# Attention front of a fused attention and two-layer MoE kernel: the order of small steps around the softmax sums, and the first inverse root moved to GpSimd

## Chip, cores and metric

One core of a Trainium2 chip (trn2) runs the whole program. The metric is the device time of one execution in microseconds. The kernel before took 538.94 us (median of 3 runs, 538.9 to 538.95).

## The reference, cut to what matters

```python
def _attn_ref(q, k, v, cap):                 # 2 x 12 heads, 448 positions, 64 wide
    scores = cap * np.tanh(scale * q @ k.T / cap)
    attn = np.exp(scores - max)
    attn = attn / (np.sum(attn, axis=-1, keepdims=True) + 1e-09)
    return attn @ v
def _moe_ref(x, w_gate, w_val, w_out, rms_g):      # x: 896 tokens x 768
    rms = np.sqrt(np.mean(x * x, axis=-1, keepdims=True) + 1e-06)
    xn = x / rms * rms_g
    return silu(xn @ w_gate) * (xn @ w_val) @ w_out
# followed by _moe2_ref: prelu(x @ w_in) @ w_out
```

The change touches the attention, and the `1 / rms` of the first batch of 448 tokens.

## The kernel before, in words

Everything is kept transposed: features on partitions, 448 tokens of a batch on the free axis. The attention is a loop over 12 head pairs (`NPAIR`), six for each batch, called **steps 0 to 11** here; step *i* computes the scores of pair *i* and finishes pair *i-1*. The order on every engine is the order in which the code calls the functions (`manual_schedule`); nothing is reordered. Each score operand is split in a high and a low part (`hi`, `lo`), so that three passes of matmuls give near full precision.

One step, by engine:

- TensorE (PE): `evac_o` frees a bank for it; then `qk_tail` (L207), `qk` for three groups (L221), `sums` of the pair before (L277: sums of the exponentials by a matrix of ones, and part of the values), `pv` of the pair before (L251). In even steps from 4 on, `norms` (L378) puts two `spread` matmuls (L372) behind the first `qk` group: they broadcast the inverse sums `r2` of two finished pairs into two banks, and `scaled` (L376) multiplies the kept values `ee` by them on VectorE, into `xf`. In step 8 the two stand ahead of the `qk` groups.
- The two banks that `spread` fills are single buffers: `under()` (tile tag u) is free once `evac_u`'s copy (L327) of the step before is done, `upper()` (tag o) once `evac_o`'s copy `ee` (L319), the first thing VectorE does in a step, is done.
- ScalarE (ACT): tanh and exp of the scores (L240, L243), and some of the weight conversion (`w_top`, L117).
- VectorE (DVE): `ee`, then `scaled`, then the lists described next, then `evac_u` (L327).
- GpSimd (POOL): sums of weight blocks (`w_sum`, L130) and, in `square` (L352 to L360), the running sum of squares of `xf`.
- SyncE (SP): issues the loads (`load_raw`, `load_v`, `w_load`), the two small DMAs `gt` of `evac_u` (L330) and the two small DMAs `r` of `recip` (L345).

Two lists per step, filled ahead of the loop, hold the rest: `first[i]` runs behind the step's softmax, `second[i]` at its end. `first` holds the loads, `prep(i+1)` (L189, two DVE instructions that split the next pair's operands), `recip` in odd steps (L332: four small DVE instructions on 64 partitions x 28, behind the landing of `gt`), and `w_bits` (L119). Before, `recip` stands behind `prep` in steps 3, 5 and 7 and ahead of it in steps 9 and 11:

```python
            steps = [(prep, i + 1)]
            if i % 2 == 1 and i > 2:
                steps.insert(i < 9, (recip, (i - 3) // 2))
```

The first batch's inverse root goes: in step 9, behind `qk_tail`, `rms_sum(0)` sums the squares over partitions on PE (L397, two matmuls into `upper("ms")`), VectorE copies the result out (L571), ScalarE takes the square root (`rms_root`, L404, with its table loaded for it and the tanh table loaded again behind it), and in step 10 VectorE takes the reciprocal (`rms_tail`, L407). `xnorm` (L418) uses the result from step 11 on. In step 10, `sums` of pair 9 stands ahead of the last `qk` group; in all other steps behind it.

Weight sums on GpSimd: `sum1` and `sum2` of group 0 and `sum1` of group 1 in steps 6 and 7; in step 8 the squares of pairs 4 and 5, then `sum2` of group 1 and `sum3` of groups 0 and 1; in step 10 the squares of pairs 6 and 7, then `sum4` of group 0.

Behind the attention, from about 97 us on, the dense layers follow (`product`, L449 and on), and PE goes from matmul to matmul to the end.

Of the kernel before, what the change touches and what calls it, by code (L numbers as in the profile page):

```python
# [7 lines left out]
F32 = mybir.dt.float32  # L8
F32R = mybir.dt.float32r
F16 = mybir.dt.float16  # L10
BF16 = mybir.dt.bfloat16
U16 = mybir.dt.uint16
U32 = mybir.dt.uint32
AF = mybir.ActivationFunctionType
ALU = mybir.AluOpType
PSUM = bass.MemoryType.PSUM
# [2 lines left out]
B, H, S, D = 2, 12, 448, 64  # L19
NP = H // 2  # L20
DM = H * D
# [12 lines left out]
RMS_EPS = 1e-6  # L34
SM_EPS = 1e-9
RP = 16
Q = 32
# [20 lines left out]
def attn_moe_kernel(ctx: ExitStack, tc: tile.TileContext, units, qk_in, v, sel, w, gvec, alpha, out):  # L58
    nc = tc.nc
# [7 lines left out]
    aconst = att.enter_context(tc.tile_pool(name="aconst", bufs=1))  # L67
    sb = att.enter_context(tc.tile_pool(name="sb", bufs=2))
# [11 lines left out]
    ones = aconst.tile([P, P], F32, name="ones")  # L80
    sel_t = aconst.tile([P, P], F32R, name="sel_t")
    r2 = [aconst.tile([P, S], F32R, name=f"r2_{i}") for i in range(2)]

# [4 lines left out]
    UW = UK * P  # L90
    tops = [const.tile([P, UW], U32, name=f"top{i}") for i in range(2)]
    raw_t, f_t, h_t, l_t = {}, {}, {}, {}
# [26 lines left out]
    def w_bits(u):  # L119
        n = width(u)  # L120
        f_t[u] = f_tile(u)[:, :n]
        nc.vector.scalar_tensor_tensor(  # L122
            out=f_t[u].bitcast(U32), in0=raw_t.pop(u).bitcast(U32)[:, 1:2 * n + 1:2], scalar=13,
            in1=top_of.pop(u), op0=ALU.logical_shift_right, op1=ALU.bitwise_or,
# [79 lines left out]
    def third():  # L204
        return ps_x.tile([P, 2, 512], F32, tag="x", name="s")
# [27 lines left out]
    def soft(i):  # L233
        t = pt[i] = sb.tile([P, TILES, S], F32, tag="pt", name="pt")
        done = 0
        for g in (*range(TG), TG) if i == 0 else (TG, *range(TG)):
            part = t[:, 2 * g:2 * g + 2] if g < TG else t[:, 2 * TG]
            if g == TG and split[i]:
                part = part.rearrange("p (h s) -> p h s", h=2)
            nc.scalar.activation(out=part, in_=st.pop((i, g)), func=AF.Tanh, scale=cinv)  # L240
            if (i, g) == (0, 1) or g == (TG if i == 0 else TG - 1):
                to = 4 if (i, g) == (0, 1) else TILES
                nc.scalar.activation(out=t[:, done:to], in_=t[:, done:to], func=AF.Exp, scale=cap_t)  # L243
                done = to
# [3 lines left out]
    def upper(name):  # L248
        return ps_o.tile([P, 512], F32, tag="o", name=name)
# [27 lines left out]
    def sums(i):  # L277

        t = pt[i]
        if i == last:  # L280
            us[i], oo[i] = (ps_s.tile([P, 2, 512], F32, tag="s", name=x)[:, 0] for x in ("us", "oo"))
        else:
            us[i] = under()
            if i:
                oo[i] = upper("oo")

        def add(h, x, k, m=slice(0, P), src=None):
            q = h + 2 * x
            nc.tensor.matmul(  # L289
                us[i][q * Q:q * Q + Q, HALF[0]], ones[m, :Q], t[m, k, src or HALF[x]], start=k == 2 * TG,  # L290
                stop=k // 2 == TG - 1, skip_group_check=True,
            )

        pv_tail(i, False)
        for h in range(2):
            for x in range(2):
                if split[i]:
                    add(h, x, 2 * TG, HEAD[x], HALF[h])
                else:
                    add(h, x, 2 * TG, HEAD[h])  # L300
        if i == 0 and split[i]:
            pv_tail(i, True)
        for n in range(2 * TG):
            for x in range(2):
                add(n % 2, x, n)
        if i and split[i]:
            pv_tail(i, True)
# [13 lines left out]
    def evac_u(i, queues=(nc.sync, nc.sync)):  # L321

        n, j = group[i]
        if j == 0:
            gt[n] = sb.tile([4 * RP, S // RP], F32, tag="gt", name="gt")
        u = sb.tile([P, S // 2], F32, tag="us", name="us")
        nc.vector.tensor_copy(u, us.pop(i)[:, HALF[0]])  # L327
        for h, q in enumerate(queues):
            r0 = 2 * RP * j + RP * h
            q.dma_start(out=gt[n][r0:r0 + RP], in_=u[h * Q:P:D].rearrange("x (p s) -> x p s", p=RP // 2))  # L330
# [16 lines left out]
    def square(i):  # L347
# [5 lines left out]
        else:  # L353
# [3 lines left out]
            else:  # L357
                nc.scalar.activation(out=sq, in_=x, func=AF.Square)
            if i < NPAIR - 2:
# [6 lines left out]
    def under():  # L366
        return ps_r.tile([P, 512], F32, tag="u", name="rps")
# [10 lines left out]
    def norms(i, *to):  # L378
        for fn in (spread, scaled):
            for j, rps in enumerate(to):  # L380
                fn(i + j, rps)
# [7 lines left out]
    rstd, spare = {}, {}  # L389

    ms_of = {}

    def rms_sum(b, ms):
        ms_of[b] = ms
        parts = s2.pop(b)
        for n, t in enumerate(parts):
            nc.tensor.matmul(ms[:, :S], ones, t, start=n == 0, stop=n == len(parts) - 1)  # L397

    def rms_keep(b):
        spare[b] = xpool.tile([P, K3, S], F32, tag="B22h", name="spare")  # L400
        rstd[b] = spare[b][:, 2]

    def rms_root(b):
        nc.scalar.activation(out=rstd[b], in_=ms_of.pop(b)[:, :S], func=AF.Sqrt, scale=1.0 / DM, bias=rms_b)  # L404

    def rms_tail(b):
        nc.vector.reciprocal(out=rstd[b], in_=rstd[b])  # L407


    oper = {}  # L410

    def first_operand(name):
# [54 lines left out]
    with tc.manual_schedule():  # L467
# [5 lines left out]
        nc.vector.memset(rms_b, RMS_EPS)  # L473
        for t in tops:
            nc.vector.memset(t, 0)
        for t in r2:
            nc.vector.memset(t.bitcast(F32), 0.0)
        hi[0] = sb.tile([P, QM], F32R, tag="hi", name="hi")
        r = sb.tile([P, QK + 1], F32, tag="rw", name="rw", bufs=2)
# [32 lines left out]
        def a(i, fn, *args):  # L512
            first.setdefault(i, []).append((fn, args))

        def z(i, fn, *args):
            second.setdefault(i, []).append((fn, args))
# [8 lines left out]
        for i in range(NPAIR):  # L525
            a(i, load_raw, i + 2)
            a(i, load_v, i + 1)
            if i == 1:
                for put, u in zip((a, z), conv[1:RAW]):
                    put(i, w_load, u)  # L530
            steps = [(prep, i + 1)]
            if i % 2 == 1 and i > 2:
                steps.insert(i < 9, (recip, (i - 3) // 2))
            for step in steps:
                a(i, *step)
            if i - 2 in range(len(conv)):
                a(i, w_bits, conv[i - 2])
                if i - 2 < len(conv) - RAW:
                    a(i, w_next, conv[i - 2])
            if i % 2 == 0 and i > 2:  # L540
                for j in range(2):
                    (a if i == 8 else z)(i, square, i - 4 + j)
            if i - 1 in range(len(conv)):
                if i < 5:
                    z(i, w_top, conv[i - 1], nc.vector.tensor_copy)
                else:
                    a(i, w_top, conv[i - 1])
        a(9, rms_root, 0)
        for n, j in ((3, 0), (4, 1), (9, 6)):
            z(n, w_hi, conv[j], nc.vector.tensor_copy)  # L550
            (a if n == 9 else z)(n + (n == 9), w_lo, conv[j])
        a(11, w_hi, conv[7])
        for put, n, fn, g in ((z, 6, sum1, 0), (z, 7, sum1, 1), (z, 7, sum2, 0), (a, 8, sum2, 1), (a, 8, sum3, 0),
                              (z, 8, sum3, 1), (z, 10, sum4, 0)):
            put(n, fn, "g", g)
        z(10, rms_tail, 0)
        a(11, xnorm, K3)
        z(11, xnorm, K3 + 1)
        for i in range(NPAIR):
            pairs = i % 2 == 0 and i > 2  # L560
            if i > 2:
                evac_o(i - 2)
            if i:
                home = {1: (ps_r, "u"), 2: (ps_o, "o")}.get(i)
                qk(i, TG, home[0].tile([P, 1, 512], F32, tag=home[1], name="s") if home else third())
            if i == 8:
                norms(i - 4, under(), upper("rps"))
            if i == 9:
                rms_sum(0, upper("ms"))
                rms_keep(0)  # L570
                nc.vector.tensor_copy(rstd[0], ms_of[0][:, :S])  # L571
                ms_of[0] = rstd[0]
            two = lambda: ps_s.tile([P, 2, 512], F32, tag="s", name="s")
            for g in range(TG - 1):
                qk(i, g, two())
                if pairs and i != 8 and g == 0:
                    norms(i - 4, under(), upper("rps"))
                if (i, g) == (1, 0):
                    oo[0] = upper("oo")
                    pv(0, range(2))  # L580
            if i == 0:
                qk(0, TG - 1, third())
                qk(0, TG, two())
            if i == 1:
                pv(0, range(2, TG))
            if i == 10:
                sums(i - 1)
            if i:
                qk(i, TG - 1, third())
            soft(i)  # L590
            for fn, args in first.pop(i, []):
                fn(*args)
            if i and i != 10:
                sums(i - 1)
            if i == 1:
                evac_o(0)
            if i:
                evac_u(i - 1)
                if i > 1:
                    pv(i - 1)  # L600
                del pt[i - 1], hi[i - 1], lo[i - 1], vt[i - 1]
            for fn, args in second.pop(i, []):
                fn(*args)
# [743 lines left out]
```

## Time and profile before

| what | value |
|---|---|
| median of 3 runs | 538.94 us |
| the profiled execution, its own time | 538.46 us |
| span of its instructions | 536.7 us |
| PE busy | 529.5 us (99%) |
| DVE, ACT, POOL busy | 448.4, 401.2, 112.0 us |

The span leaves 1.8 us around it. PE is the engine to look at: its busy time and its idle time together are the span, so the kernel is shorter only where PE waits less or does less. An idle engine beside it costs nothing until PE, or something in PE's way, waits for it.

### The profile page before, as it was taken

How to read it: one execution, taken by the hardware profiler on the slowest of the kernel's cores; microseconds unless marked ns; L12 is line 12 of the kernel's file. 1: busy time of each engine (PE TensorE's matmuls, PEld its weight loads, DVE VectorE, ACT ScalarE, POOL GpSimd, SP SyncE). 2: the span in 40 equal slices, each digit the busy share in tenths (PEclk: the TensorE clock that was granted, in tenths of full speed). 3: DMA queues.
4: the chain of work that ended last, by engine and by line, in shares of the span. 5: the costliest groups of instructions: out<-in, count | busy, mean ns of one | idle time of the engine just before them, and what ended most of it. 6: DMA issues, size and time to landing. Idle time of an engine off the chain costs nothing.

```text
span 536.7 us, 8344 instructions
## 1 busy us (share of the span) xinstructions
PE 529.5 (99%) x3322; PEld 450.9 (84%) x3322; DVE 448.4 (84%) x516; ACT 401.2 (75%) x475; POOL 112.0 (21%) x80
## 2 busy tenths in 40 slices
PE   8999999999999999999999999999999999999997
PEld 5554544799999999999999999999999999999996
DVE  5588889898999968789789796959997897998951
ACT  7989989577766665477788776789989996995530
POOL 0023763400066441010023011110310131210000
PEclk9999999999999999999999999999999999999999
DMA  6856520400334526048866769334466689564111
GB/s 213 317 174 228 180 77 11 160 18 2 117 118 176 174 87 211 0 177 253 274 179 111 165 205 299 66 59 131 174 231 230 207 233 203 97 144 112 51 53 51
DMA packets 22343, 80.05 MB, mean 149 GB/s; under 512 B 3744, under 2 KB 6688, under 8 KB 22304
## 3 DMA queue, kind: packets, MB, share of 16 engines
q1 hardware_dynamic: 16378, 65.43, 35.2%
q0 software_dynamic: 5552, 13.70, 14.0%
q8 instruction: 26, 0.43, 0.3%
q10 hardware_dynamic: 374, 0.39, 0.2%
q14 instruction: 13, 0.11, 0.1%
HBM read 62.99 MB, written 2.75 MB: 123 GB/s over the span
## 4 chain that ended last, share of the span: by engine, by line
PE 89%; DVE 5%; ACT 2%; POOL 2%; DMA 1%; issue 0%; DVEq 0%; SPq 0%
PE s L449 19%; PE x L449 13%; PE m L449 13%; PE s L825 8%; PE x L825 7%; PE s L795 6%; PE x L795 5%; PE m L825 4%; PE m L795 3%; PE oo L256 2%; PE s L229 2%; PE rps L289 2%; PE s L461 1%; ACT pt L243 1%; PE oo L272 1%; DVE wt L122 1%
## 5 line engine op out<-in xcount | busy, mean ns | idle before, releaser
L143 DVE TENSOR_TENSOR wl<-wt,wh 128x768 fp32r<-128x768 f32 x109 | 111.7, 1026 | 20.4 <-ACT wh L137 20.1
L137 ACT CAST wh<-wt 128x768 fp32r<-128x768 f32 x106 | 87.9, 832 | 39.8 <-PE s L825 9.1
L130 POOL TENSOR_TENSOR wt<-wt 128x768 f32<-128x768 f32 x25 | 58.4, 2341 | 163.6 <-DVE wl L143 75.7
L117 ACT CAST top<-raw 128x768 f16<-128x768 bf16 x64 | 68.9, 1077 | 20.2 <-DMA raw<-w_in 9.0
L122 DVE SCALAR_TENSOR_TENSOR wt<-raw,top 128x768 uint32<-128x768 uint32 x64 | 66.9, 1047 | 1.1 <-ACT top L117 1.1
L449 PE MATMUL s<-xx,wh 128*128 128x448 f32 x264 | 63.7, 365 | 0.0
L671 DVE TENSOR_TENSOR xx<-b,xx 128x896 fp32r<-128x896 f32 (+1 forms) x55 | 62.3, 1139 | 0.0
L449 PEld LDWEIGHTS s<-xx,wh 128*128 128x128 f32 x264 | 49.3, 187 | 4.8 <-issue 0.9
L449 PE MATMUL x<-xx,wh 128*128 128x448 f32 x204 | 49.9, 366 | 0.0
L449 PE MATMUL m<-xx,wh 128*128 128x448 f32 x204 | 49.5, 364 | 0.0
L892 POOL DMA_DIRECT2D wt<-wt x25 | 22.0, 880 | 126.1 <-DVE wt L122 62.6
L240 ACT ACTIVATE pt<-s,cinv 128x896 f32<-128x896 f32 (+1 forms) x48 | 41.0, 911 | 4.6 <-PE s L229 2.3
L449 PEld LDWEIGHTS x<-xx,wh 128*128 128x128 f32 x204 | 38.2, 187 | 3.5 <-issue 0.4
L825 PE MATMUL s<-xx,wh 128*128 128x448 f32 x144 | 40.9, 364 | 0.0
L449 PEld LDWEIGHTS m<-xx,wh 128*128 128x128 f32 x204 | 38.2, 187 | 3.0
L825 PE MATMUL x<-xx,wh 128*128 128x448 f32 x128 | 36.3, 364 | 0.0
L243 ACT ACTIVATE pt<-pt,cap_t 128x3136 f32<-128x3136 f32 (+2 forms) x13 | 35.3, 2714 | 0.4
L449 PE MATMUL s<-xx,wl 128*128 128x448 f32 x132 | 33.8, 364 | 0.0
L795 PE MATMUL s<-xx,wh 128*128 128x448 f32 x108 | 30.7, 364 | 0.0
L256 PE MATMUL oo<-pt,vt 128*32 128x448 f32 x288 | 29.5, 540 | 0.4 <-ACT pt L243 0.4
L825 PEld LDWEIGHTS s<-xx,wh 128*128 128x128 f32 x144 | 27.0, 188 | 1.9
L1186 ACT CAST xx<-b 128x896 fp32r<-128x896 f32 x28 | 26.4, 943 | 1.2 <-DVE b L671 1.1
(204 smaller groups left out, 1122.7 us busy)
## 6 DMA issues: line engine op xcount, KB each, us to landing
raw<-w_in SPq DMA_DIRECT2D x68, 768.0 KB
wt<-wt POOLq DMA_DIRECT2D x25, 384.0 KB, 4.7
rw<-qk_in SPq DMA_DIRECT2D x11, 480.0 KB
vt<-v_in SPq DMA_DIRECT2D x12, 288.0 KB
lent<-wt POOLq DMA_DIRECT2D x5, 384.0 KB, 7.5
b<-b POOLq DMA_DIRECT2D x4, 448.0 KB, 5.7
out<-P SPq DMA_DIRECT2D x5, 224.0 KB
out<-b SPq DMA_DIRECT2D x2, 448.0 KB
```

The costliest lines, as they stand in the source:

```text
L117: copy(top_of[u].bitcast(F16)[:, 1::2], raw_t[u].bitcast(BF16)[:, 4:4 * n + 4:4])
L122: nc.vector.scalar_tensor_tensor(out=f_t[u].bitcast(U32), in0=raw_t.pop(u).bitcast(U32)[:, 1:2 * n + 1:2], scalar=13, in1=top_of.pop(u), o ...
L130: add(out=t, in0=f_t[a], in1=f_t[b], op=op)
L137: copy(h_t[u], f_t[u].rearrange("p (k m) -> p k m", m=P))
L143: nc.vector.tensor_tensor(out=l_t[u], in0=f_t[u].rearrange("p (k m) -> p k m", m=P), in1=h_t[u], op=ALU.subtract)
L240: nc.scalar.activation(out=part, in_=st.pop((i, g)), func=AF.Tanh, scale=cinv)
L243: nc.scalar.activation(out=t[:, done:to], in_=t[:, done:to], func=AF.Exp, scale=cap_t)
L256: nc.tensor.matmul(oo[i][q * Q:q * Q + Q, :S], vv[:, n, q % 2 * Q:q % 2 * Q + Q], t[:, n, :], start=i == c == 0, stop=i > 0 and c == TG - ...
L449: nc.tensor.matmul(ps[:, r, :S], lhs, rhs, start=first and n == 0, stop=n == len(mm) - 1, skip_group_check=True,)
L671: nc.vector.tensor_tensor(out=out, in0=a, in1=b, op=op)
L795: nc.tensor.matmul(dst[m], wt[:, kk * MB + m, :], x, start=first and u == 0 and kk == 0 and n == 0, stop=u == UO - 1 and kk == 1 and n == ...
L825: nc.tensor.matmul(dst[m], wt[:, kk * MB + m, :], x, start=first and u == kk == i == 0, stop=last and kk == 1 and i == 2, skip_group_check ...
```

## The change

Step numbers as above. It

- puts `recip` ahead of `prep` in steps 3, 5 and 7 too;
- in step 6 puts `sums(5)` and `evac_u(5)` ahead of `w_bits` (on PE their place stays; on VectorE and SyncE they come earlier);
- in step 10 puts `sums(9)` back behind the last `qk` group;
- on GpSimd moves `sum2` of group 0 from step 7 to step 8, behind the squares, and `sum3` of group 1 to step 9;
- in step 9 puts `rms_sum(0)` behind the first `qk` group, and in place of the copy, the square root on ScalarE and the reciprocal on VectorE: a copy of 32 rows (`root_begin`), a DMA of one row to a tile of 16 partitions x 28, a scale on GpSimd, two integer instructions on VectorE (the usual first guess of an inverse root), four Newton steps of four instructions on GpSimd, the split in two parts there, and four DMAs from SyncE to rows of a new tile `rr` (`root_small`, at the start of `second[9]`, ahead of `sum3` of group 1 on GpSimd);
- in step 11, behind the first `qk` group, broadcasts `rr` by one matmul and copies it out on VectorE (`root_end`);
- clears `rr` once at the start on VectorE.

```diff
+    rr = aconst.tile([D, S], F32R, name="rr")
...
+    def root_begin(ms):
+        u = sb.tile([Q, S], F32, tag="sq", name="mrow", bufs=2)
+        nc.vector.tensor_copy(u, ms[:Q, :S])
+        nc.sync.dma_start(out=tiny_tile("x"), in_=u[:1].rearrange("h (p s) -> h p s", p=RP))
+
+    def root_small():
+        x, y, t = small["x"], tiny_tile("y"), tiny_tile("t")
+        ts, mul = nc.gpsimd.tensor_scalar, lambda o, a, b: nc.gpsimd.tensor_tensor(out=o, in0=a, in1=b, op=ALU.mult)
+        ts(out=x, in0=x, scalar1=1.0 / DM, scalar2=RMS_EPS, op0=ALU.mult, op1=ALU.add)
+        nc.vector.tensor_scalar(
+            out=t.bitcast(U32), in0=x.bitcast(U32), scalar1=1, scalar2=None, op0=ALU.logical_shift_right
+        )
+        nc.vector.tensor_scalar(
+            out=y.bitcast(I32), in0=t.bitcast(I32), scalar1=-1.0, scalar2=float(0x5F3759DF), op0=ALU.mult, op1=ALU.add
+        )
+        for _ in range(4):
+            mul(t, y, x)
+            mul(t, t, y)
+            ts(out=t, in0=t, scalar1=-0.5, scalar2=1.5, op0=ALU.mult, op1=ALU.add)
+            mul(y, y, t)
+        th, tl = tiny_tile("th", F32R), tiny_tile("tl", F32R)
+        nc.gpsimd.tensor_copy(th, y)
+        nc.gpsimd.tensor_tensor(out=tl, in0=y, in1=th, op=ALU.subtract)
+        for r0, part in enumerate((th, tl)):
+            for r in (r0, r0 + Q):
+                nc.sync.dma_start(
+                    out=rr[r:r + 1].rearrange("r (p s) -> r p s", p=RP).bitcast(F32), in_=part.bitcast(F32)
+                )
+
+    def root_end(ps):
+        nc.tensor.matmul(ps[:, :S], sel_t[:D], rr, start=True, stop=True, skip_group_check=True)
+        rms_keep(0)
+        nc.vector.tensor_copy(rstd[0], ps[:, :S])
...
-        for t in r2:
+        for t in (*r2, rr):
             nc.vector.memset(t.bitcast(F32), 0.0)
...
-                steps.insert(i < 9, (recip, (i - 3) // 2))
+                steps.insert(0, (recip, (i - 3) // 2))
             for step in steps:
                 a(i, *step)
             if i - 2 in range(len(conv)):
+                if i == 6:
+                    a(i, sums, i - 1)
+                    a(i, evac_u, i - 1)
                 a(i, w_bits, conv[i - 2])
...
-        a(9, rms_root, 0)
+        z(9, root_small)
+        z(9, sum3, "g", 1)
...
-        for put, n, fn, g in ((z, 6, sum1, 0), (z, 7, sum1, 1), (z, 7, sum2, 0), (a, 8, sum2, 1), (a, 8, sum3, 0),
-                              (z, 8, sum3, 1), (z, 10, sum4, 0)):
+        for put, n, fn, g in ((z, 6, sum1, 0), (z, 7, sum1, 1), (a, 8, sum2, 0), (a, 8, sum2, 1), (a, 8, sum3, 0),
+                              (z, 10, sum4, 0)):
             put(n, fn, "g", g)
-        z(10, rms_tail, 0)
...
-            if i == 9:
-                rms_sum(0, upper("ms"))
-                rms_keep(0)
-                nc.vector.tensor_copy(rstd[0], ms_of[0][:, :S])
-                ms_of[0] = rstd[0]
...
+                if (i, g) == (11, 0):
+                    root_end(upper("rps"))
+                if (i, g) == (9, 0):
+                    rms_sum(0, upper("ms"))
+                    root_begin(ms_of.pop(0))
...
-            if i == 10:
-                sums(i - 1)
```

The last lines of the diff, left out, make the two exceptions to the place of `sums` and `evac_u` (step 10 before, step 6 now).

## Rows read from the trace of the kernel before

**Rows 1.** The page, part 1: TensorE's busy time.

```profile
PE 529.5 (99%) x3322; PEld 450.9 (84%) x3322; DVE 448.4 (84%) x516; ACT 401.2 (75%) x475; POOL 112.0 (21%) x80
```

**Rows 2.** Timeline of PE: start us, length us, what, [idle before <- releaser].

```profile
32.64 0.36 PE L372 MATMUL rps<-r,sel_t 64*128 64x448 f32 x2
...
47.16 0.36 PE L372 MATMUL rps<-r,sel_t 64*128 64x448 f32 x2
...
53.21 0.61 PE L219 MATMUL s<-rw 64*64 64x224 f32 x8
...
61.13 0.47 PE L372 MATMUL rps<-r,sel_t 64*128 64x448 f32 x2 [0.30 <-DMA r<-tl]
...
69.33 1.02 PE L397 MATMUL ms<-s,ones 128*128 128x448 f32 x2 [0.92 <-POOL s L360]
...
78.50 0.47 PE L372 MATMUL rps<-r,sel_t 64*128 64x448 f32 x1 [0.15 <-DVE ee L319]
...
85.13 0.61 PE L219 MATMUL s<-rw 64*64 64x224 f32 x8
...
87.38 0.47 PE L229 MATMUL s<-hi 64*128 64x448 f32 x2 [0.22 <-ACT pt L240]
...
97.48 0.88 PE L449 MATMUL s<-xx,wh 128*128 128x448 f32 x3
```

**Rows 3.** Timeline of DVE at the start of the program.

```profile
2.67 0.91 DVE L477 MEMSET r<- 128x448 f32 x2
3.95 0.23 DVE L496 CAST hi<-rw 128x128 fp32r<-128x128 f32 x1 [0.38 <-DMA rw<-qk_in]
```

**Rows 4.** Timeline of DVE in step 3.

```profile
24.71 0.58 DVE L195 CAST hi<-rw 128x832 fp32r<-128x832 f32 x1
...
26.80 0.23 DVE L337 TENSOR_SCALAR gf<-gt,eps_t 64x28 f32<-64x28 f32 x1 [0.45 <-DMA gt<-us]
...
29.27 0.39 DVE L327 COPY us<-rps 128x224 f32<-128x224 f32 x1 [0.59 <-PE rps L289]
...
31.55 0.62 DVE L319 COPY ee<-oo 128x448 f32<-128x448 f32 x1
```

**Rows 5.** Timeline of DVE in step 5 and at the start of step 6.

```profile
43.30 0.23 DVE L337 TENSOR_SCALAR gf<-gt,eps_t 64x28 f32<-64x28 f32 x1 [0.34 <-DMA gt<-us]
...
46.05 0.63 DVE L319 COPY ee<-oo 128x448 f32<-128x448 f32 x1 [0.57 <-PE oo L256]
```

**Rows 6.** Timeline of SP, the last small DMA ahead of step 8.

```profile
59.22 0.57 SPq L345 DMA_DIRECT2D r<-tl  x1
```

**Rows 7.** Timeline of POOL.

```profile
0.24 0.10 POOL L1337 MEMSET const-float32-0.0<- 128x1 f32 x1 [0.24 <-issue]
...
63.27 1.28 POOL L356 TENSOR_TENSOR sq<-xf 128x448 f32<-128x448 f32 x1
64.63 1.81 POOL L360 TENSOR_TENSOR s<-s,sq 128x448 f32<-128x448 f32 x1
...
69.23 5.41 POOL L130 TENSOR_TENSOR wt<-wt 128x768 f32<-128x768 f32 x3
79.09 0.93 POOL L352 TENSOR_TENSOR s<-xf 128x448 f32<-128x448 f32 x1 [4.45 <-DVE xf L376]
```

**Rows 8.** Timeline of DVE in steps 9 and 10, and at the last `xnorm` ahead of the product.

```profile
70.38 0.62 DVE L571 COPY spare<-ms 128x448 f32<-128x448 f32 x1 [1.82 <-PE ms L397]
...
72.92 1.76 DVE L342 TENSOR_TENSOR tl<-gf,th 64x28 fp32r<-64x28 f32 x1
...
77.03 0.42 DVE L327 COPY us<-rps 128x224 f32<-128x224 f32 x1
...
77.80 0.65 DVE L319 COPY ee<-oo 128x448 f32<-128x448 f32 x1
78.39 1.25 DVE L376 TENSOR_TENSOR xf<-ee,rps 128x448 f32<-128x448 f32 x2
...
96.40 1.21 DVE L427 CAST xx<-xf 128x448 fp32r<-128x448 f32 x1
```

More of the change, by code (lines that the diff above doesn't have):

```diff
@@ L13 @@
 U32 = mybir.dt.uint32
+I32 = mybir.dt.int32
 AF = mybir.ActivationFunctionType
@@ L407, in rms_tail, with tiny_tile @@
         nc.vector.reciprocal(out=rstd[b], in_=rstd[b])
+    small = {}
+    def tiny_tile(name, dt=F32):
+        small[name] = aconst.tile([RP, S // RP], dt, name=name)
+        return small[name]
+    def root_begin(ms):
[29 more added lines that the diff above has]
+        nc.vector.tensor_copy(rstd[0], ps[:, :S])
     oper = {}
@@ L592, in attn_moe_kernel @@
                 fn(*args)
-            if i and i != 10:
+            if i and i != 6:
                 sums(i - 1)
@@ L597, in attn_moe_kernel @@
             if i:
-                evac_u(i - 1)
+                if i != 6:
+                    evac_u(i - 1)
                 if i > 1:
```

## The prediction

> **What bounds the kernel now.** I read the page first, then the timeline of PE, then the engines beside it around each wait of PE. The page shows PE busy for 529.5 of 536.7 us [rows 1], so only the 7 us in which it is idle, and work added to it, can move the end; behind the attention it waits for nothing, so a shift there reaches the end whole. The timeline of PE [rows 2] shows four waits that the change aims at: 0.30 us for the DMA of the inverse sums in step 8, 0.92 us for GpSimd's squares in step 9, 0.15 us for the copy `ee` in step 10, 0.22 us for a tanh in step 11. Together 1.6 us is all there is to win, unless PE does less. The reader should then look at what stands just behind each wait: where VectorE is nearly as late as PE, a wait removed comes back one step on.
>
> **The start.** One clear more on VectorE, 0.46 us (two took 0.91). It stands in front of a cast that sat idle for 0.38 us before its DMA landed [rows 3]. The difference, **0.1 us**, is on the path to the first scores.
>
> **`recip` ahead of `prep`, steps 3 and 5.** `recip` cannot begin before the DMA of the sums is in: VectorE waits for it for 0.45 us in step 3 even with `prep` in front, which ran from 24.71 to 26.35 [rows 4]. The DMA does not come sooner in these steps, since nothing ahead of it moves. So VectorE idles while it could have done `prep`, and does `prep`, 1.6 us, afterwards. In step 3 an idle time of 0.59 us ahead of `us` takes a part; the rest, 1.0 us, goes on to `ee`, which follows without a gap and ends at 33.2 instead of 32.17 [rows 4]. The second `spread` needs the bank that `ee` frees, and PE starts it at 32.64 now [rows 2]: **0.55 us** of new wait. Step 5 has the same shape: 1.6 us less the 0.57 us that `ee` waits for PE today; `ee` ends at 47.7 instead of 46.68 [rows 5], the `spread` now at 47.16 [rows 2] waits **0.55 us**. What is queued behind the waiting instruction is all of VectorE's step. Bounds: 0 (if VectorE makes it up) to 0.6 each.
>
> **Steps 7 and 8.** Here the DMA does come sooner, as `evac_u(5)` moves ahead of `w_bits`, and ahead of a weight load on SyncE's queue; so `recip` ahead of `prep` costs nothing in step 7 (without that cover it would cost what it does in step 3). The last DMA, issued at 59.22, let PE go at 61.13, 1.9 us later [rows 2, 6]; sooner by more than 0.30, it leaves PE waiting for `ee` of step 8 alone, which ends just before. I take **-0.15** (0 to -0.30).
>
> From here I use the clock of before; the 1.2 us so far moves all engines alike.
>
> **Step 9.** On GpSimd a weight sum of 1.8 us (three in 5.41 us) goes from ahead of the squares to behind them [rows 7]. The squares can't start before `xf` of step 8, which is ready about 1.1 us behind the `spread` at 61.13 (in step 10: 78.50 to 79.64), so at 62.2 instead of 63.27: GpSimd is 1.1 us ahead, the squares are done at 68.1 and the three sums behind them at 73.5 instead of 74.64 [rows 2, 7, 8]. PE would ask for them at 69.33 - 0.92 - 0.15 = 68.26, and one group of scores later, 0.7 us ((87.38 - 85.13 - 0.22 - 0.61) / 2), at 68.97 [rows 2]. No wait is left, and VectorE's copy of the sum starts at 70.0 instead of 70.38 [rows 8].
>
> **What is late next: `ee` of step 10.** VectorE's chain from that copy to `ee` is as long as PE's step. In it the subtraction `tl` took 1.76 us and ended at 74.68, as GpSimd's third sum did at 74.64 [rows 7, 8]; another small operation on 64 x 28 took 0.23 us [rows 5]. So the two engines shut each other out for whole instructions. With GpSimd 1.1 us earlier `tl` ends 1.1 us earlier; the two integer instructions add 0.2 us each. `ee` ends at 78.45 - 1.1 + 0.4 = 77.75, and `spread` runs at 77.8 instead of 78.50: **-0.7**, not -1.2. From `spread` to the next step took 6.05 us where nothing waited and `sums` stood behind the last group (47.16 to 53.21) [rows 2]; so step 11 starts at 83.85 instead of 85.13, **-1.28** in all since step 8. ScalarE's square root with its two table loads falls away and hides nothing; VectorE's reciprocal too. With them away the tanh that `sums` was moved ahead of is no longer late, so its order goes back at no cost (0.22 us, as in step 11, if it is).
>
> **The Newton chain.** Its scale on GpSimd waits for SyncE's row DMA (issued about 70.6, behind the copy; two pair loads now queue behind it, wanted a step later) and for the sums, until 73.5. VectorE's two integer instructions come behind `us`: 75.95 + 0.3, done at 76.65. Then 18 GpSimd instructions, each needing the one before. No row shows one of 16 x 28. Below: a clear of one column, 0.10 us. Above: 448 columns with two inputs, 0.93 us, and 0.08 us between two that depend on each other (64.55 to 64.63) [rows 7]. I take 0.10 + 0.06 (28 of 448 columns of 0.93) + 0.08 = **0.24 us**, near the small row. Where they run follows from the shutting out. VectorE's weight copy holds GpSimd back until 77.15. While `ee` and `xf` read PSUM, which did not stop a square at 79.09 (0.93 us beside `xf` at 78.39) [rows 7, 8], 7 fit until 78.95. Then one each goes between the two parts of `prep` (1.6 us) and a weight subtraction of about 1.0 us, until 82.0. VectorE is then idle, and the 17th (`th`) is done at 82.0 + 7 x 0.24 = 83.7. SyncE needs 0.57 us an issue and a landing 1.9 us [rows 2, 6]: the fourth DMA is issued at 85.4 and lands at **87.3**.
>
> PE asks for it at 83.85 + 1.3 (tail and one group) = 85.15. It **waits 2.15 us**, with all of step 11 behind it. One matmul more costs 0.2 us (0 to 0.47), and the wait of 0.22 us for a tanh goes [rows 2]. Since step 8: -1.28 + 2.15 + 0.2 - 0.22 = **+0.85**.
>
> By the Trainium skill (GPSIMD Engine Reference, section 3.1) a two-input operation takes 2.6 cycles an element at 1.2 GHz and 4497 ns for 2048; that leaves 0.06 us fixed, so 0.12 us here, 0.20 us with the gap. By that estimate the DMA would land at 86.6 and the forecast would be 540.6.
>
> **Behind it.** `sum3`, squares and `sum4` are wanted only by the dense layers, but on GpSimd they now run behind the chain, in step 11, against VectorE's `recip` and `xnorm`; SyncE's four DMAs stand ahead of the values of pair 11 and the sums that this `recip` waits for. One shut-out like `tl`'s costs 1.5 us. The last `xnorm` half ends at 97.61 [rows 8] and the product's third matmul wants it about 0.4 us behind 97.48 [rows 2]: slack of 0.3, plus 0.85 by which PE is later. I take **+0.35** (0 to 0.9).
>
> **Sum:** 0.1 + 1.1 + 0.85 + 0.35 = 2.4 us; the 0.15 of step 8 is inside the 1.28. The profiled execution had 538.46 us, 1.76 beyond its span, and stands 0.48 below the median; on the median 538.94 + 2.4 = **541.3 us**.
>
> **Rivals.**
> - *The chain is hidden.* Below about 0.13 us an instruction, 15 fit until 78.95 and the rest between VectorE's next three; the DMA lands before 85.15. The 2.15 and the 0.35 go, the matmul stays, and the squares press on `prep` as they do now (0.2): 539.0, not slower. For it speaks the clear of 0.10 us, against it that these have two inputs and depend on each other. 0.17.
> - *VectorE makes up steps 3 and 5* (something ahead of `gt` is quicker): 1.1 us less, 540.2. The idle times read are too small for it. 0.10.
> - *Both*: the mends win what they aim at, 537.8, faster. 0.10.
> - *The chain is twice as long* (0.4 us each): 4 until 78.95, 3 more until 82.6, the 17th at 86.6, the DMA lands at 90.2: 2.9 more, 544.2. It may also start late: GpSimd's scale has 2.7 us to spare (73.5 to 76.25), beyond which VectorE waits, and `ee` and PE behind it. 0.18.
>
> On late starts the Trainium skill (GPSIMD Engine Reference, section 2.1) says that the first call of a freshly loaded GpSimd kernel costs about 6 us; no run here shows one for a scale. By that estimate the time would be 3.2 us above the forecast, 544.5.
>
> **How the numbers follow.** The forecast has 0.45. The 538.4 to 543.9 range leaves out the faster case (0.10) and the far half of the long chain; an instruction as long as 448 columns (1.01 us) would give some 552 and lies outside. A measurement of this kernel tells about 0.2%, 1.1 us, from no change: 537.9 to 540.0 is the same. Faster: 0.10 and 0.03 from the edge of the hidden chain. Same: 0.14 of it, half of the second rival, and 0.03 of the forecast's low edge: 0.22. Slower: the rest, 0.65.
>
> **What would show it.** On PE: waits of half a microsecond at `spread` in steps 4 and 6 with `ee` as the releaser, none at the squares' sum, the new matmul of step 11 waiting 2 us for a DMA. On GpSimd: 18 small instructions 0.24 us apart, fewer beside `prep`. If PE never waits for `rr`, the forecast is wrong; if steps 4 and 6 are as long as before, its second largest term is.

## The result and the profile after

| | before | after |
|---|---|---|
| median, runs side by side | 538.95 us (4 runs) | 542.09 us (4 runs) |
| the profiled execution, its own time | 538.46 us | 542.05 us |
| span | 536.7 us | 540.3 us |
| PE busy | 529.5 us | 532.1 us |

The ratio is 1.006, 95% interval 1.0048 to 1.0072: **slower by 3.1 us**. The forecast was 541.3 us.

The page of the changed kernel, part 1, beside [rows 1]: PE is busy for 2.6 us longer, with one more matmul, which takes 0.63 us. So some matmuls became longer.

```profile
PE 532.1 (98%) x3323; PEld 452.8 (84%) x3323; DVE 444.8 (82%) x519; ACT 398.7 (74%) x472; POOL 116.8 (22%) x99
```

The timeline of PE of the changed kernel, at the places of [rows 2] and at the beginnings of more steps (L221 is the first matmul of a step, L374 `spread`, L399 the squares' sum, L450 the new matmul of the root, L494 the product; `...` stands for lines left out):

```profile
33.00 0.36 PE L374 MATMUL rps<-r,sel_t 64*128 64x448 f32 x2
...
48.01 0.47 PE L374 MATMUL rps<-r,sel_t 64*128 64x448 f32 x2 [0.28 <-DVE ee L321]
...
54.14 0.61 PE L221 MATMUL s<-rw 64*64 64x224 f32 x8
...
61.70 0.75 PE L374 MATMUL rps<-r,sel_t 64*128 64x448 f32 x2
...
70.01 1.02 PE L399 MATMUL ms<-s,ones 128*128 128x448 f32 x2
...
78.07 0.89 PE L374 MATMUL rps<-r,sel_t 64*128 64x448 f32 x2
...
84.56 0.61 PE L221 MATMUL s<-rw 64*64 64x224 f32 x8
...
88.37 0.63 PE L450 MATMUL rps<-rr,sel_t 64*128 64x448 f32 x1 [2.39 <-DMA rr<-tl]
88.38 0.99 PE L231 MATMUL s<-hi 64*128 64x448 f32 x2
88.87 0.87 PE L231 MATMUL s<-hi,lo 64*128 64x448 f32 x2
...
95.92 0.46 PE L374 MATMUL s<-r,sel_t 64*128 64x448 f32 x1
...
100.76 0.47 PE L494 MATMUL s<-xx,wh 128*128 128x448 f32 x1
```

Held against [rows 2], PE's lateness goes +0.36 us (33.00), +0.93 (54.14), -0.57 (84.56), +3.28 (100.76). No idle time stands any more at 61.70, 70.01 or 78.07, and the tanh of step 11 is waited for no longer. But the wait for `ee` is hidden rather than gone. The two matmuls of `spread` at 33.00 start together and take 0.36 us; the pair at 61.70 takes 0.75 us and the pair at 78.07 takes 0.89, since the second of each starts only when VectorE's copy `ee` is done, while the first still runs or has just ended. The second matmul of the later pair, then the two copies, with VectorE's `wl` behind them:

```profile
78.50 0.47 PE L374 MATMUL rps<-r,sel_t 64*128 64x448 f32 x1
```

```profile
61.30 0.62 DVE L321 COPY ee<-oo 128x448 f32<-128x448 f32 x1 [0.87 <-PE oo L258]
...
77.84 0.60 DVE L321 COPY ee<-oo 128x448 f32<-128x448 f32 x1
...
81.11 1.00 DVE L145 TENSOR_TENSOR wl<-wt,wh 128x768 fp32r<-128x768 f32 x1
```

Step 10 takes 7.74 us (76.82 to 84.56), where step 4, with its pair together, takes 7.31.

Two new losses follow. The first is the wait of 2.39 us for the last DMA of the root. The second stands right behind it: the scores behind it start 0.37 to 0.49 us apart, where pairs of such matmuls otherwise take 0.20 (85.41 to 85.61 us, just ahead of the wait).

The table by stretch of the changed kernel shows why (columns: stretch, its length, busy time of PE, PEld, DVE, ACT and POOL, granted clock, DMA share, GB/s):

```profile
86.00:88.00 2.00, 0.00 (x0) 0.00 (x0) 0.00 (x0) 1.01 (x1) 2.00 (x3) 1.00 0.03 3
88.00:90.00 2.00, 1.63 (x10) 1.66 (x12) 0.62 (x1) 0.00 (x0) 1.92 (x3) 0.61 0.54 149
90.00:92.00 2.00, 2.00 (x23) 0.84 (x19) 1.51 (x3) 1.72 (x2) 1.51 (x1) 0.53 0.00 0
92.00:94.00 2.00, 2.00 (x48) 1.27 (x44) 1.90 (x6) 1.97 (x2) 0.00 (x0) 1.00 0.03 4
```

PE did nothing from 86 to 88 us. From 88.5 to 91.9 us the granted clock was at its lower level, 1.2 GHz, and the scores ran in that stretch. From the root's matmul to the next `spread` PE took 95.92 - 88.37 = 7.55 us. Where the clock stayed up the same work took 6.09 us (93.28 - 86.93 - 0.26, three Newton steps, below). **So the slow matmuls cost 1.46 us.** The low clock is there in every execution: the mean granted clock of the four timed ones is 0.994 to 0.996 of full speed, and that of the kernel before, in all its executions beside the experiments, 0.998 to 1.0.

| stretch of PE | us against before |
|---|---|
| start | +0.37 |
| step 6, first matmul of step 6 to that of step 7 (7.84 against 7.30) | +0.54 |
| steps 7 to 10 (+0.93 to -0.57) | -1.50 |
| wait for rr | +2.39 |
| slow matmuls behind it | +1.46 |
| step 5, the new matmul less the tanh wait that went, and rounding | +0.02 |
| sum at the product | +3.28 |

The two profiled executions are 3.59 us apart; the last 0.3 us come behind the product and are not followed here.

The chain of the root on GpSimd and its DMAs on SyncE, in the changed kernel:

```profile
74.91 0.21 POOL L428 TENSOR_SCALAR x<-x 16x28 f32<-16x28 f32 x1 [0.73 <-DMA x<-mrow]
77.60 0.41 POOL L427 TENSOR_TENSOR t<-y,x 16x28 f32<-16x28 f32 x1 [2.49 <-DVE y L432]
78.09 0.24 POOL L427 TENSOR_TENSOR t<-t,y 16x28 f32<-16x28 f32 x1
78.42 0.20 POOL L438 TENSOR_SCALAR t<-t 16x28 f32<-16x28 f32 x1
...
80.28 1.01 POOL L427 TENSOR_TENSOR y<-y,t 16x28 f32<-16x28 f32 x1
81.36 0.84 POOL L427 TENSOR_TENSOR t<-y,x 16x28 f32<-16x28 f32 x1
...
84.72 0.23 POOL L442 TENSOR_TENSOR tl<-y,th 16x28 fp32r<-16x28 f32 x1
```

```profile
84.67 1.21 SPq L445 DMA_DIRECT2D rr<-th  x2
85.97 1.16 SPq L445 DMA_DIRECT2D rr<-tl  x2
```

Three things are to be read here. (An operation has 16 x 28 = 448 numbers.) The scaled row was ready at 75.12 us, and GpSimd then stood for 2.49 us until VectorE came to its two integer operations. An operation takes 0.20 to 0.24 us, and the next starts about 0.3 us after the start of the one before; beside VectorE's `lo` and `wl` single ones take 1.01 and 0.84 us. The four DMAs go out one behind another, 0.6 us each.

### The profile page after: what moved, and what is told of

Read it like the earlier page. It is cut to its first block, busy times and chain, and to the rows that moved or that the text cites. A ratio compares the mean times of both kernels' runs of the same rounds, so it can differ in the third digit from the quotient of the medians.

```text
span 540.3 us, 8374 instructions
## 1 busy us (share of the span) xinstructions
PE 532.1 (98%) x3323; PEld 452.8 (84%) x3323; DVE 444.8 (82%) x519; ACT 398.7 (74%) x472; POOL 116.8 (22%) x99
## 4 chain that ended last, share of the span: by engine, by line
PE 91%; DVE 3%; DMA 2%; ACT 1%; POOL 1%; issue 1%; SPq 0%; DVEq 0%; POOLq 0%
PE s L494 19%; PE m L494 13%; PE x L494 13%; PE s L872 8%; PE x L872 7%; PE s L842 6%; PE x L842 5%; PE m L872 4%; PE oo L258 3%; PE m L842 3%; PE s L231 3%; PE rps L291 2%; PE s L506 1%; PE oo L274 1%; DVE wt L124 1%
## 5 line engine op out<-in xcount | busy, mean ns | idle before, releaser
L494 PE MATMUL s<-xx,wh 128*128 128x448 f32 x264 | 63.6, 365 | 0.0
L494 PEld LDWEIGHTS s<-xx,wh 128*128 128x128 f32 x264 | 49.3, 187 | 4.8 <-issue 0.9
L494 PE MATMUL x<-xx,wh 128*128 128x448 f32 x204 | 49.9, 366 | 0.0
L494 PE MATMUL m<-xx,wh 128*128 128x448 f32 x204 | 49.6, 364 | 0.0
L494 PEld LDWEIGHTS x<-xx,wh 128*128 128x128 f32 x204 | 38.2, 188 | 3.5 <-issue 0.4
L494 PEld LDWEIGHTS m<-xx,wh 128*128 128x128 f32 x204 | 38.2, 188 | 3.2 <-issue 0.2
L872 PE MATMUL x<-xx,wh 128*128 128x448 f32 x128 | 36.3, 364 | 0.0
L494 PE MATMUL s<-xx,wl 128*128 128x448 f32 x132 | 33.8, 364 | 0.0
L842 PE MATMUL x<-xx,wh 128*128 128x448 f32 x96 | 27.2, 364 | 0.0
```

Source lines behind the costliest of these rows:

```text
L494: nc.tensor.matmul(ps[:, r, :S], lhs, rhs, start=first and n == 0, stop=n == len(mm) - 1, skip_group_check=True,)
L842: nc.tensor.matmul(dst[m], wt[:, kk * MB + m, :], x, start=first and u == 0 and kk == 0 and n == 0, stop=u == UO - 1 and kk == 1 and n == ...
L872: nc.tensor.matmul(dst[m], wt[:, kk * MB + m, :], x, start=first and u == kk == i == 0, stop=last and kk == 1 and i == 2, skip_group_check ...
```

## The experiments

Each was timed beside the kernel before on the same chip, at 538.76 or 538.77 us. The diffs are cut to the lines that matter.

**1. Half the Newton chain.**

```diff
-        for _ in range(4):
+        for _ in range(2):
```

> The changed kernel with two of the four Newton steps left out (so the first inverse root is less exact): 8 of the 18 GpSimd instructions of the chain fall away, 8 x 0.31 us = 2.5 us, as much as TensorE waits for the last small DMA in step 11 (2.39 us). Theory A (the slow clock behind the wait is the wait's own doing): the wait and the 3.4 us at half clock behind it both go, 2.4 + 1.45 us: 538.2 us. Rival B (the wait alone goes, the slow clock comes from something else in step 11, such as the 64-row matmul or the pile of small work): 539.7 us, with matmuls of 0.58 to 0.9 us still behind the new matmul.

Measured: 538.56 us, ratio 0.9991 (0.9983 to 1.0). In its timeline PE has no wait at the root's matmul, and the clock is at its upper level all through:

```profile
85.64 0.44 PE L450 MATMUL rps<-rr,sel_t 64*128 64x448 f32 x1
...
92.02 0.44 PE L374 MATMUL s<-r,sel_t 64*128 64x448 f32 x1 [0.30 <-DMA r<-tl]
```

The late root is what makes the change slow: without it 3.5 us are gone. The second line shows what is late next, the inverse sums for the last `spread` of step 11; the DMAs of `gt` that they need stand behind those of `rr` on SyncE's queue (experiment 9 takes two of these away).

**2. The clear alone, in the kernel before.**

```diff
-        for t in r2:
+        for t in (*r2, rr):
```

> The kernel before with nothing but one more clear of 64 x 448 on VectorE at the start. Theory A (the clear makes the first scores late enough that TensorE's clock rises later, at about 6.5 us instead of 4): 538.95 + 0.37 = 539.3 us, with first score matmuls of 0.58 us instead of 0.37. Rival B (the clear costs its own 0.1 us, the late clock was chance): 539.05 us.

Measured: 538.80 us, ratio 0.9998 (0.999 to 1.0007). No difference is seen, but the interval, -0.54 to +0.38 us, holds both theories. The profiles don't decide either. PE reached its upper clock 4.0 us into the execution before, 6.5 in the one after, 7.2 in this one and 4.9 with the mends alone (below), which has no clear. The first matmul of step 1 starts at 16.21 to 16.31 us in the three profiled kernels without the clear and at 16.30 to 16.79 in the nine with it. So how much of the 0.37 us at the start belongs to the clear stays open.

**3. Inverse sums behind the split again, in steps 3 and 5 only.**

```diff
-                steps.insert(0, (recip, (i - 3) // 2))
+                steps.insert(i in (3, 5), (recip, (i - 3) // 2))
```

> The changed kernel with the small reciprocal back behind prep in steps 3 and 5 only (step 7 as changed). Theory A, read from the two traces (step 4 cost nothing, step 6 cost 0.46 us): 542.09 - 0.46 = 541.6 us. Rival B, the forecast's term (0.55 us in each of steps 4 and 6): 541.0 us. In both, PE's wait of 0.28 us for the copy ee in step 6 is gone.

Measured: 541.75 us, ratio 1.0057 (1.0045 to 1.0069). In its profile step 6 is as long as before (7.31 us), and the wait for `rr` is 2.38 us again. The saving against the changed kernel, 0.34 us, is of the size expected, but not beyond the scatter of the runs. What the profiles show better is why step 6 varies. With `recip` ahead of `prep` its length was 7.84, 7.87, 7.70, 7.80, 7.39 and 7.30 us in six kernels with that order. With the order of before it was 7.30 to 7.32 in four, and 7.76 and 8.30 in two (experiments 9 and 4b) where PE waited for the DMA of `r`. With `recip` first it follows the landing of `gt`: from the issue of its two DMAs to `gf` 4.15 us in the changed kernel, 3.83 and 3.79 us in the two short ones. VectorE waits for that DMA, and everything it has to do for the step waits behind.

**4. The mends of order alone, with the old root.** The changed kernel with the square root on ScalarE in step 9 and the reciprocal on VectorE in step 10, as before.

```diff
-        z(9, root_small)
+        a(9, rms_root, 0)
+        z(10, rms_tail, 0)
...
-                if (i, g) == (11, 0):
-                    root_end(upper("rps"))
```

> The changed kernel with the first root as it was (square root on ScalarE in step 9, reciprocal on VectorE in step 10) and without the new tile: the changes of order alone. Theory A (the order needs ScalarE free: with the square root and its two table loads, 3.3 us, ahead of step 10's first tanh, the last group of scores waits some 1.4 us for it, as sums no longer stand in front): 539.5 to 540.2 us. Rival B (the order alone wins what it aims at): 538.0 us, with no wait of TensorE over 0.3 us in step 10.

Measured: 538.93 us, ratio 1.0003 (0.9994 to 1.0011). Both theories miss: A is 0.6 us too high, B 0.9 too low. The timeline shows the waits moved, not gone:

```profile
78.23 0.46 PE L374 MATMUL rps<-r,sel_t 64*128 64x448 f32 x1 [0.50 <-DVE us L329]
79.23 0.47 PE L374 MATMUL rps<-r,sel_t 64*128 64x448 f32 x1 [0.54 <-DVE ee L321]
```

PE reached step 10 early and stood there for VectorE, twice, so that the matmuls of step 11 begin at 85.39 us, no earlier than in the kernel before (85.13).

**4b. The same with the order of before in steps 3 and 5.** With the order of experiment 3 in steps 3 and 5 as well:

> The run with the mends of order alone and the old root of ScalarE and VectorE (538.93 us), with one edit: in steps 3 and 5 the inverse sums behind the split again. Theory A (of the mends only the one in step 5 costs anything before step 7, and it costs 0.46 us): TensorE's matmuls of step 7 start 0.4 us earlier, and as nothing behind waits for a fixed time 538.5 us. Theory B (the waits in step 10, 0.50 and 0.54 us for VectorE, and in step 11 take it back, since VectorE's queue sets them): 538.9 us.

Measured: 538.57 us, 0.9995 (0.9986 to 1.0004). Its two waits in step 10 are the same 0.50 and 0.54 us. The medians lean to theory A, but the two intervals overlap, and the profiled execution is the slowest of the eleven (539.36 us, step 6 of 8.30 us): open.

**5. Three Newton steps.** `range(3)` in the line of experiment 1.

> The changed kernel with three Newton steps instead of four; nothing else moves (the root leaves out its last refinement). In the changed kernel's trace one step is four GpSimd operations 0.32 us apart, so the rows of rr should land 1.28 us earlier and TensorE's wait ahead of the root's spreading matmul should shrink from 2.39 to about 1.1 us. Theory A (the low clock behind the wait is the wait's own consequence and comes only behind a long one): the granted clock stays at its upper level behind the shorter wait, and both the 1.28 us of wait and the 1.45 us of slow matmuls go: 542.1 - 2.7 = 539.4 us. Theory B (any stop there brings the low clock, or the low clock belongs to that place of the program): the stretch at half clock is still there, and only the wait is saved: 542.1 - 1.3 = 540.8 us.

Measured: 539.56 us, ratio 1.0013 (1.0004 to 1.0021). Theory A. One step, 1.25 us of wait, took 2.5 us with it. The timeline of PE: behind a wait of 1.14 us the scores take 0.54 us, no longer 0.87.

```profile
86.93 0.44 PE L450 MATMUL rps<-rr,sel_t 64*128 64x448 f32 x1 [1.14 <-DMA rr<-tl]
...
87.25 0.54 PE L231 MATMUL s<-hi,lo 64*128 64x448 f32 x2
...
93.28 0.44 PE L374 MATMUL s<-r,sel_t 64*128 64x448 f32 x1 [0.26 <-DMA r<-tl]
```

**6. Six Newton steps.** `range(6)`.

> The changed kernel with six Newton steps instead of four (two more, which add nothing to the root). Eight more GpSimd operations 0.32 us apart: the wait for rr should grow from 2.39 to about 4.95 us. Theory A (the low clock is one stretch of fixed length behind a long wait): the matmuls behind it are slow for as long as before, about 3.4 us, and the time is 542.1 + 2.6 = 544.7 us. Theory B (the slow stretch grows with the wait before it, here by the same factor of two): a further 1.5 us, 546.2 us. If something else than the arrival of rr set the end of the wait, the time would stay at 542.1 us.

Measured: 544.64 us, ratio 1.0105 (1.0091 to 1.0119). The time is that of theory A, its mechanism only in part. The timeline of PE and two stretches of the table:

```profile
90.33 0.71 PE L450 MATMUL rps<-rr,sel_t 64*128 64x448 f32 x1 [4.86 <-DMA rr<-tl]
...
98.49 0.47 PE L374 MATMUL s<-r,sel_t 64*128 64x448 f32 x1
```

```profile
88.00:90.00 2.00, 0.00 (x0) 0.00 (x0) 0.00 (x0) 0.00 (x0) 2.00 (x3) 0.57 0.03 3
...
92.00:94.00 2.00, 2.00 (x23) 0.88 (x19) 1.65 (x3) 1.69 (x2) 1.45 (x1) 0.50 0.00 0
```

The wait is 4.86 us as forecast. The clock fell while PE was still waiting, and stayed low until 95.1 us: the root's matmul to `spread` took 8.16 us, so 2.07 us were lost to it, where the changed kernel lost 1.46. The loss does grow, though not by the factor of theory B. In this execution step 6 was 0.45 us shorter than in the changed kernel's profile, which hides it in the sum.

**7. The root's matmul one group of scores later.** Four steps, the wait partly covered.

```diff
-                if (i, g) == (11, 0):
+                if (i, g) == (11, 1):
                     root_end(upper("rps"))
```

> The changed kernel with one edit: in step 11 the root's spreading matmul stands one group of scores later in TensorE's order, so that 0.62 us of scores and ScalarE's tanh go ahead of it. Four Newton steps as before. The rows of rr land at the same time, so the wait ahead of the matmul should shrink from 2.39 to about 1.8 us; the other scores behind it, 0.62 us, cover less of VectorE's copy of the root, for which the next matmuls into that bank wait, some 0.5 us. Theory A (the clock falls only behind a wait longer than the 1.8 us that is left; it stayed up behind 1.14 us): no stretch at half clock, 542.1 - 1.45 - 0.1 = 540.5 us. Theory B (1.8 us with another 0.5 us close behind is enough): the stretch is there again, 541.5 to 542.0 us.

Measured: 540.38 us, ratio 1.0032 (1.002 to 1.0045). Theory A: the chain is as long as in the changed kernel, and 1.7 us are gone. PE waits 1.76 us, and the clock stays up (1.00 in every stretch from 82 to 98 us):

```profile
87.58 0.44 PE L450 MATMUL rps<-rr,sel_t 64*128 64x448 f32 x1 [1.76 <-DMA rr<-tl]
...
87.89 0.54 PE L231 MATMUL s<-hi,lo 64*128 64x448 f32 x2
...
93.93 0.44 PE L374 MATMUL s<-r,sel_t 64*128 64x448 f32 x1 [0.68 <-DMA r<-tl]
```

Not all of the 1.7 us is the clock's and the wait's. From the first matmul of step 11 to `spread` PE took 10.14 us (83.79 to 93.93), 1.22 less than in the changed kernel (84.56 to 95.92); step 6 happened to be 0.54 us shorter in this execution (7.30 against 7.84).

**8. The chain shortened.** Three Newton steps, the scaling and the two integer operations (`root_seed`) ahead of the weight operation of step 9, steps 3 and 5 as before.

```diff
+            if i == 9:
+                a(i, root_seed)
             if i - 2 in range(len(conv)):
```

> The changed kernel with three edits: three Newton steps instead of four, the root's scaling and its two VectorE integer operations put into step 9 ahead of the first weight operation there (they waited on VectorE until 77.1 us while the scaled row was ready at 75.1 us), and in steps 3 and 5 the inverse sums behind the split again, as in the kernel before. Theory A (the chain of the root is the whole cost, and step 6 the rest): chain 1.3 + 1.3 us earlier, wait for rr under 0.4 us, clock at its upper level throughout, step 6 without the 0.46 us; against the run with two Newton steps (538.56 us) another 0.46 us: 538.1 us, faster than the kernel before by about 0.7 us. Theory B (what steps 8 to 11 gain is given back at the waits for later steps' inverse sums, at 92 and 102 us, since those chains hang on VectorE's order): the earlier arrival only lengthens these waits, and the time is 538.5 to 538.8 us.

Measured: 538.82 us, ratio 1.0002 (0.9993 to 1.0011). Theory B's time, though not only by its reason: the wait for `rr` was still 0.51 us (an operation of 0.82 us and three slow ones beside `prep` and `wl` ate most of the gain: the first DMA of `rr` went out 14.44 us behind the first matmul of step 9, with three Newton steps alone 14.77), the inverse sums at 92.8 us cost 0.29, and PE's idle time before `ee` of step 10 grew to 0.38 us, from 0.07.

**9. Two DMAs instead of four.** Experiment 8, with each part of the root in one row, spread by ones.

```diff
-            for r in (r0, r0 + Q):
-                nc.sync.dma_start(
-                    out=rr[r:r + 1].rearrange("r (p s) -> r p s", p=RP).bitcast(F32), in_=part.bitcast(F32)
-                )
+            nc.sync.dma_start(
+                out=rr[r0:r0 + 1].rearrange("r (p s) -> r p s", p=RP).bitcast(F32), in_=part.bitcast(F32)
+            )
...
-        nc.tensor.matmul(ps[:, :S], sel_t[:D], rr, start=True, stop=True, skip_group_check=True)
+        nc.tensor.matmul(ps[:, :S], one_r, rr, start=True, stop=True, skip_group_check=True)
```

> The run with the seed early (538.82 us) with one more edit: each part of the inverse root goes into one row of rr instead of two, and is spread over all partitions by a constant of ones, so that two transfers stand on SyncE's queue instead of four. At 0.58 to 0.6 us of SyncE for each, the last part should be under way 1.2 us earlier, and the sums of step 10, whose transfers stand behind them on that queue, too. Theory A (these two waits, 0.51 us for rr and 0.29 us for the inverse sums at 92.8 us, are what keeps the seed-early run from being faster than the kernel before): both go, 538.0 to 538.3 us, faster than the kernel before by 0.1 to 0.15%. Theory B (the 0.38 us that the early integer operations cost at step 10's spread, and the waits behind 100 us, take it back): 538.5 to 538.9 us, no difference that a measurement of this kernel can tell.

Measured: 537.86 us, ratio 0.9984 (0.9975 to 0.9993). **Faster than both kernels**: 4.2 us below the changed one, 0.9 below the one before. The interval does not reach 1, though the gain is under the 0.2% that the prediction counts as faster. It is a little more than theory A had, of whose two waits only one went. The timelines of PE and SP:

```profile
85.52 0.36 PE L454 MATMUL rps<-rr,one_r 64*128 64x448 f32 x1
...
91.97 0.44 PE L375 MATMUL s<-r,sel_t 64*128 64x448 f32 x1 [0.43 <-DMA r<-tl]
```

```profile
82.48 0.57 SPq L449 DMA_DIRECT2D rr<-th  x1
83.15 0.55 SPq L449 DMA_DIRECT2D rr<-tl  x1
```

The root's matmul waits for nothing. The wait for the inverse sums of step 11 did not go as expected (0.43 us): VectorE's `th` of that `recip` took 1.40 us beside GpSimd's weight sum and ended 0.03 us behind it. That is what is late next. In the profiles step 10 is also 0.27 us shorter than in experiment 8 (7.79 against 8.06), so the step from 538.82 to 537.86 us is not all the two DMAs' doing.

## Why the prediction was right

The direction, the place and the largest term held: the mends gain, and PE then waits for the DMA of the root with all of step 11 behind it. The time came out 0.8 us above the forecast, since one loss was not foreseen and two smaller ones did not come. So the sum is nearer than its terms, and that is luck. By its own steps:

- **Wait for rr**: predicted 2.15 us, measured 2.39. Its parts were less right than the sum. The pitch of 0.24 us was too small: single operations stand 0.3 us apart. But the three operations that I had put between VectorE's whole instructions ran stretched beside them, so that VectorE was done with `wl` at 82.11 us, not at 82.0 + 0.93, and the chain began at 77.60, not at 77.15 + 0.93. By luck these errors cancelled: `th` was done at 84.64 us (84.44 + 0.20), where I had 83.7 on the clock of before, 84.6 with the 0.93 us of lateness. Experiments 1, 5 and 6 show that the chain sets this wait: each Newton step moves it by 1.2 us.
- **By the Trainium skill** (GPSIMD Engine Reference, section 3.1) I had 0.12 us for an operation and 0.20 with the gap. The rows of the changed kernel show 0.20 to 0.24 for the operation alone: the measurement decides, and the sum by the page, 540.6, is farther off. Of the 6 us that the Trainium skill (GPSIMD Engine Reference, section 2.1) gives for a first call no row shows anything: the scale took 0.21 us.
- **Since step 8**: predicted -1.28, measured -1.50 in steps 7 to 10. VectorE came earlier as argued, by a little more: `ee` of step 10 ended at 78.44 us (77.84 + 0.60), where I had 77.75 + 0.93 = 78.68. As the prediction had it, this copy still sets the pace of step 10: the second matmul of `spread` started behind it, at 78.50, and step 11 began 6.06 us later (6.05 predicted).
- **Step 6**: predicted 0.55, measured 0.54 in this execution, but 0 to 0.57 in others (experiment 3). The term was right for a DMA that lands as late as in the profile of before.
- **Step 4**: predicted 0.55, measured none in this execution. "The DMA does not come sooner in these steps" was the step that failed. The issues of `gt` on SyncE's queue, before and after, and the timeline of DVE of the changed kernel, beside [rows 4]:

```profile
22.33 1.08 SPq L330 DMA_DIRECT2D gt<-us  x2
```

```profile
22.68 1.09 SPq L332 DMA_DIRECT2D gt<-us  x2
```

```profile
26.46 0.23 DVE L339 TENSOR_SCALAR gf<-gt,eps_t 64x28 f32<-64x28 f32 x1 [1.32 <-DMA gt<-us]
...
29.82 0.40 DVE L329 COPY us<-rps 128x224 f32<-128x224 f32 x1
...
32.09 0.62 DVE L321 COPY ee<-oo 128x448 f32<-128x448 f32 x1
```

  `gf` started 0.34 us earlier than before although all else was 0.36 later, so `ee` ends at 32.71, in time for the `spread` at 33.00. From the issue to `gf` it was 4.47 us before and 3.78 after. That looks like scatter: with the same order it was 4.17 us in experiment 5 and 4.30 in experiment 7, and there step 4 did take longer, 7.51 and 7.63 us against 7.31. Step 5 then gave most of it back (7.05 and 7.02 us against 7.25).
- **Behind the chain**: predicted +0.35 at the product, measured none. From `spread` to the product PE took 4.84 us in both kernels (95.92 to 100.76 after). The loss that I feared is there in the runs with the chain whose clock stayed up, at another place: in experiments 1, 5, 7, 8 and 9 PE waits 0.26 to 0.68 us for the inverse sums just ahead of that `spread`, and behind it the product is 4.84 to 4.85 us away again. With the slow stretch (the changed kernel, experiments 3 and 6) this wait is absent. So PE's own slowness seems to have covered it.
- **The start**: predicted 0.1; experiment 2 can't tell it from nothing, nor from 0.37.
- **Not foreseen**: 1.46 us of slow matmuls. I priced a wait by its own length. Experiments 5 and 7 shorten the wait in two different ways, from the chain's end and from PE's, and both bring the clock back.

Of the rivals, the hidden chain (539.0) is what experiment 1 made: 538.56. That VectorE makes up steps 3 and 5 (540.2) held for step 3 in this execution. A time like that of the mends winning what they aim at (537.8) needed the shorter chain of experiment 9, with steps 3 and 5 as before: 537.86. A chain half as long again, as experiment 6 made it, gave 544.64, what I had for one twice as long.

## What to carry to other kernels

A chain of many tiny dependent operations, with DMAs in and out, is priced by its pitch and by what runs beside it, and its place is right only if its end lies ahead of the moment at which PE asks. Where PE must wait, put work that doesn't need the result ahead of the waiting matmul: what is saved can be more than the wait. Before moving an instruction that waits for a DMA ahead of one that doesn't, look at the idle time in front of it: what stood there was its cover. A landing time read from one execution is one draw: here it ran from 3.8 to 4.5 us for the same small DMA.

## What was not expected of the hardware

**A wait of PE can cost more than its length.** The granted clock, and what PE did before:

| wait of PE | granted clock behind it | root's matmul to `spread`, without its wait |
|---|---|---|
| 1.14 us (experiment 5) | 2.4 GHz | 6.09 us |
| 1.76 us (experiment 7) | 2.4 GHz | not alike, a group of scores stands ahead |
| 2.39 us (after) | 1.2 GHz from 88.5 to 91.9 us | 7.55 us |
| 2.38 us (experiment 3) | 2.4 GHz for 1.6 us, then 1.2 GHz from 89.4 to 92.8 us | 7.62 us |
| 4.86 us (experiment 6) | 1.2 GHz from 88.3 to 95.1 us | 8.16 us |

Behind two waits of equal length the fall came at once in one execution and 1.6 us later in the other, at nearly the same cost. What a wait of one of these lengths does at another place, no run here shows.

**The first rise of the clock varies**: 4.0 to 7.2 us into the execution, in twelve profiled kernels that differ little at the start. Step 1 began between 16.21 and 16.79 us in them. No run separates the clock's part from that of the clear, but a term read from one profile carries this scatter with it.

**Single small operations become several times as long beside the other of VectorE and GpSimd**: 0.23 us to 1.01 us for one of 448 numbers on GpSimd, and 0.17 to 1.40 us for `th` on VectorE. In the cases looked at, they end just behind a large instruction of the other engine, as if held until it is done. In the changed kernel the weight sum below ends at 91.51 us and `gf`, 0.23 us long elsewhere, at 91.55; the GpSimd operation of 1.01 us ends 0.10 us behind `lo`, that of 0.84 us 0.09 behind `wl`.

```profile
89.69 1.82 POOL L132 TENSOR_TENSOR wt<-wt 128x768 f32<-128x768 f32 x1
```

```profile
90.42 1.13 DVE L339 TENSOR_SCALAR gf<-gt,eps_t 64x28 f32<-64x28 f32 x1 [0.76 <-DMA gt<-us]
```
